# The last product of each column block in two feed-forward layers, over 128 rows of stacked weights instead of 64

## The chip, the cores and the metric

One Trainium2 chip, one core of it. The metric is the device time of one execution of the whole program in microseconds (us); lower is better. Engines are called by their short names: PE (matrix products; PEld is its loading of weights), DVE (vector), ACT (scalar), POOL (gpsimd) and SP (which issues most transfers).

## What is computed

Three layers follow one another: a linear recurrence over 768 steps for 4 batches of 8 heads, a dense feed-forward over its output, and a routed feed-forward with 8 experts.

```python
for t in range(S):                                   # 768 steps, 4 batches, 8 heads of 40
    y[:, :, t] = einsum('bhd,bhde->bhe', rt, state)
    Sa = einsum('bhde,bhe->bhd', state, at)
    state = state * wt[:, :, None, :] - einsum('bhd,bhe->bhde', Sa, bt) + einsum('bhd,bhe->bhde', vt, kt)
x = y.transpose(0, 2, 1, 3).reshape(3072, 320)
h = x @ w_in                                         # 320 -> 2048
g = where(h > 0, h, exp(min(h, 0)) - 1)
x = g @ w_out                                        # 2048 -> 320
...                                                  # gate and expert of each token
h = maximum(einsum('ecd,edf->ecf', disp, w1), 0.0)   # 8 experts, 320 -> 1024
y = einsum('ecf,efd->ecd', h, w2)                    # 1024 -> 320
out[i] = gate_w[i] * y[expert_idx[i], pos[i]]
```

## The kernel before

**Two parts of every number.** Products are made in float32r, a type of float32 width that keeps fewer digits. So that the result has float32's accuracy, an operand x is split into H (x rounded to float32r) and L (the rest), by `split`: ACT makes H, DVE makes L. A product of two split operands is wH xH + wH xL + wL xH; wL xL is left out.

**The first layer of each feed-forward.** The 320 features on the contraction side are two blocks of 128 and one of 64. For a column block of 128 hidden features the two full blocks take three products each: six. For the block of 64 the weights are stacked: `wiS` (`w1S` in the routed layer) holds wH in its rows 0 to 63 and wL in its rows 64 to 127, and x has its last 64 features twice (columns 320 to 383 repeat 256 to 319 before they are turned), so rows 64 to 127 of xH and of xL repeat rows 0 to 63. One product of `wiS` with xH over 128 rows then gives wH xH + wL xH, and one more, with xL, gives wH xL: eight products for a column block, added up in one bank of the accumulator. The dense layer's are written in `first` inside `Moe1.block` (line 581 issues them), the routed layer's in `Moe2.first` (line 901).

**Stages.** In the first 224 us or so weights are converted and the first chunks of the recurrence prepared. Then `body` goes through 12 pairs of chunks (a chunk is 32 steps of all 32 heads). In pair p it weaves together the recurrence of the two chunks (`chain`, `pre`, `inverse`: many small products in PE tiles of 32, 40, 64 or 104 rows, with DVE, ACT and POOL between them and transfers through memory) and `Moe1.block(p - 1)`, the dense layer on 256 tokens of the pair before: 16 column blocks f, each `first(f)`, then for its successors `second` with lines 595 to 597. After the last pair come its block alone, the first 256 tokens of expert 0 (`early`), and the eight experts (`expert`), each 8 column blocks of up to 448 tokens (`first`), then 3 or 4 groups of tokens (`second`, lines 907 to 909, and lines 1000 and 1001 for a group of 64), whose rows `put` scatters to the output with POOL's indirect transfers. Rows of the next expert's tokens are gathered by POOL too (line 941) and turned by PE (line 962).

**Order.** A scheduler places the instructions of every engine in a fixed order when the program is built (`ahead` lifts the recurrence over the dense layer), and each engine runs its own list in that order, waiting on semaphores of the others. So a product that could run early stands still behind one that waits.

The lines of `first` that the change touches, and those that issue the products:

```python
            for kt in range(2):
                seq += [(self.wiH[:, kt, fs], xH[:, kt]), (self.wiH[:, kt, fs], xL[:, kt]),
                        (self.wiL[:, kt, fs], xH[:, kt])]
            seq += [(self.wiS[:, fs], xH[:, 2]), (self.wiS[0:64, fs], xL[0:64, 2])]
            for i, (l, r) in enumerate(seq):
                nc.tensor.matmul(h, l, r, start=i == 0, stop=i == len(seq) - 1)
```

Of the kernel before, what the change touches and what calls it, by code (L numbers as in the profile page):

```python
# [30 lines left out]
S0 = 448  # L31
EARLY = 256
# [6 lines left out]
class Attention:  # L39
    """Chunks of 32 steps of the recurrence, all 32 heads at a time.  # L40

    In a chunk, with W the running product of w, A = W(t-1) a, Bt = b / W, Kt = k / W:
    (I + T) P = A S0' + M V with T, M the strictly lower parts of A Bt', A Kt';
    Y = W(t-1) (R S0 - low(R P') Bt + low(R V') Kt); S = (S0 - P' Bt + V' Kt) W(end).
    """

# [79 lines left out]
    def lanes(self, g, eng, eng2=None, room=None):  # L126
        """Running products and scaled operands of chunks 4g..4g+3: a lane is a chunk of a head.

        W holds 1, w, ... and then the reciprocals, running backward; room: a second such tile,
        and tiles for b and k."""  # L130
        nc = self.nc
# [22 lines left out]
        yield  # L154
        # products in 4 blocks of 8, then of the blocks
        eight = lambda t: t.rearrange("p (q r) d -> p q r d", r=8)
# [49 lines left out]
    def load_heads(self, t, src, hg, s0, n):  # L206
        """Rows of an input, n steps on partitions, the 16 heads of half hg side by side."""
        self.nc.sync.dma_start(
            t[:, :, 0:40], src[2 * hg:2 * hg + 2, :, s0:s0 + n, :].rearrange("b h s d -> s (b h) d"))

    def load_tok(self):
        """The next operand that is turned, rows of 16 heads."""
        if self.loaded == len(self.order):
            return
        kind, i = self.order[self.loaded]
        t = self.t("tok", self.loaded)
        self.loaded += 1
        for hg in range(2):
            rows = t[64 * hg:64 * hg + 64]
            if kind == "r":  # L220
                self.load_heads(rows, self.src["r"], hg, 64 * i, 64)
            elif kind == "a":
                for cc in range(2):
                    lane = (2 * (i % 2) + cc) * 32 + 16 * hg
                    self.nc.sync.dma_start(  # L225
                        rows[32 * cc:32 * cc + 32, :, 0:40],
                        self.scr_A[i // 2][lane:lane + 16].rearrange("l s d -> s l d"))
            else:
                lane = (i % 4) * 32 + 16 * hg
                self.last = self.nc.sync.dma_start(  # L230
                    rows[:, :, 0:40], self.scr_BK[i // 4][lane:lane + 16].rearrange("l x d -> x l d"))
# [28 lines left out]
    def pre(self, p):  # L260
        """Scaled operands of chunks 2p, 2p+1, features on partitions; T and M of both."""
        nc = self.nc
# [36 lines left out]
    def inverse(self, p):  # L299
        """(I + T)^-1 of chunks 2p, 2p+1, transposed: a lane for the even, one for the odd rows of each head and chunk."""  # L300
        nc = self.nc
# [7 lines left out]
        for j in range(31):  # L309
            # column j + 1, that the next step waits for, goes between the others' two operations  # L310
            n, m = j // 2 + 1, 30 - j
            if m:
                tv = self.t("ut", j)[:, 0:n * m].rearrange("p (a b) -> p a b", a=n)
                nc.vector.tensor_tensor(  # L314
                    tv, TL[:, j:j + 1, j + 2:32].to_broadcast([128, n, m]),
                    UL[:, 0:n, j:j + 1].to_broadcast([128, n, m]), ALU.mult,
                )
            col = UL[:, 0:n, j + 1]
            nc.vector.scalar_tensor_tensor(col, UL[:, 0:n, j], TL[:, j, j + 1:j + 2], col, ALU.mult, ALU.add)  # L319
            if m:  # L320
                nc.vector.tensor_tensor(UL[:, 0:n, j + 2:32], UL[:, 0:n, j + 2:32], tv, ALU.add)  # L321
            if j % 2 == 1:
                yield
# [24 lines left out]
    def bank(self, c):  # L348
        """Three banks by turns; the third has other work in the first chunks."""
        self.banks += 1  # L350
        return self.psum("r" if c >= 6 and self.banks % 3 == 0 else "c")

    def warm(self, c):
        """Products of constants, so that the tensor engine's clock stays up in the first chunks."""
        if c < 2:
# [5 lines left out]
    def chain(self, c, put):  # L361
# [12 lines left out]

        # S' and what is left of the last chunk come first
        if cc == 0:
# [91 lines left out]
def split(nc, H, L, x, low=None):  # L468
    """x = H + L: H rounded to float32r, L the rest."""
    split.last = nc.scalar.copy(H, x)  # L470
# [3 lines left out]
class Moe1:  # L474
# [9 lines left out]
    def weights(self, pool, route):  # L484
        """float64 words to float32r parts, a column block at a time; w_out w_gate beside w_out."""
        nc = self.nc
# [64 lines left out]
    def put_x(self, ident, psum):  # L551
        """x of a chunk, [tokens, features], to features on partitions, in two parts."""
        nc = self.nc
# [11 lines left out]
    def block(self, p, done):  # L565
        """Tokens of chunks 2p, 2p+1; done(c, psum) takes what comes out, [tokens, features]."""
        nc = self.nc
# [4 lines left out]
        def first(f):  # L572
# [3 lines left out]
            for kt in range(2):  # L576
                seq += [(self.wiH[:, kt, fs], xH[:, kt]), (self.wiH[:, kt, fs], xL[:, kt]),
                        (self.wiL[:, kt, fs], xH[:, kt])]
            seq += [(self.wiS[:, fs], xH[:, 2]), (self.wiS[0:64, fs], xL[0:64, 2])]
            for i, (l, r) in enumerate(seq):  # L580
# [34 lines left out]
class Router:  # L615
    """Expert and gate of each token, and each expert's list of tokens."""

# [37 lines left out]
    def settle(self):  # L655
        """From here on tokens take places from EARLY on: what is before stays as it is."""
        nc = self.nc
# [46 lines left out]
    def counts(self):  # L704
        """Places of each expert, the most of any of them."""
        nc = self.nc
# [10 lines left out]
    def overflow(self, ctx, w1, w2, out, psum):  # L717
        """Experts with more than S0 tokens: the rest of their tokens, 128 at a time."""
        nc, tc = self.nc, self.tc
# [39 lines left out]
    def drop(self, ctx, out, psum, capacity):  # L759
        """Tokens that come after their expert's capacity is filled get zeros."""  # L760
        nc, tc = self.nc, self.tc
        pool = ctx.enter_context(tc.tile_pool(name="drop", bufs=1))
        t = lambda shape, name, dt=F32: pool.tile(shape, dt, tag=name, name=name)
        # [k, m] = 1: same batch, earlier step; same batch; earlier batch
        step, same, less = t([128, 128], "step", BF16), t([128, 128], "same", BF16), t([128, 128], "less", BF16)
# [32 lines left out]
class Moe2:  # L798
# [20 lines left out]
    def weights(self, e):  # L819
        """Weights of an expert in two parts."""  # L820
        nc = self.nc
# [22 lines left out]
    def early(self, ctx, psum):  # L844
        """The first EARLY places of expert 0, in the room of expert 1's weights."""
        nc = self.nc
# [9 lines left out]
        nc.gpsimd.memset(xs, 0.0)  # L856
        # rows that are still to come
        for b in range(B):
# [34 lines left out]
    def first(self, f, h, w, xH, xL):  # L893
# [3 lines left out]
        for k in range(2):  # L897
            seq += [(w1H[:, k, fs], xH[:, k]), (w1H[:, k, fs], xL[:, k]), (w1L[:, k, fs], xH[:, k])]
        seq += [(w1S[:, fs], xH[:, 2]), (w1S[0:64, fs], xL[0:64, 2])]
        for i, (l, r) in enumerate(seq):  # L900
# [24 lines left out]
    def groups(self, e):  # L925
        """Number, first place and size of the groups of places of an expert that are still to be done."""
        return [(j, at, n) for j, (at, n) in enumerate(SLOTS) if e or at >= EARLY]

    def load(self, e):
        """Token list of an expert, and the rows of those tokens."""  # L930
        nc = self.nc
# [16 lines left out]
    def turn(self, e):  # L948
        """Rows of an expert, features on partitions, in two parts."""
        nc = self.nc  # L950
# [18 lines left out]
    def expert(self, e, turn, weights):  # L969
# [5 lines left out]
        hs = self.pool.tile([128, NF2, 2 * S0], F32R, tag="hs", name="hs", bufs=2)  # L975
        # the second part begins with the last 64 places
        hH, hL, hM = hs[:, :, 0:S0], hs[:, :, S0 + 64:2 * S0], hs[:, :, S0:S0 + 64]
# [8 lines left out]
        if turn is not None:  # L986
            drain(turn)
        # the pair that takes an addition not last of all
        for j, at, n in g if e + 1 < E else g[:1] + g[3:] + g[1:3]:
# [5 lines left out]
            else:  # L995
                # both parts of h side by side: the halves of y are added up
                w2H, w2L = w[3:5]
# [18 lines left out]
def ahead(tc, g, offset):  # L1016
    """The generator's instructions, offset places earlier for the scheduler."""
    while True:
# [8 lines left out]
def weave(*gens):  # L1027
    """Runs generators side by side, each (generator, steps[, first step]) at its own pace, all to their end."""
    state = [[g, n, at[0] if at else 0, True] for g, n, *at in gens]
# [168 lines left out]
```

## Time and profile before

| | |
|---|---|
| median of 3 runs | 1390.91 us |
| lowest and highest run | 1386.13 and 1399.85 us |
| span of the profiled execution, first to last instruction | 1384.7 us |
| median run less that span | 6.2 us |
| busy PE, PEld, DVE, ACT, POOL | 1122.0, 958.8, 780.7, 606.7, 315.7 us |
| mean granted clock of PE | 0.909 of full speed |

No separate time of the profiled execution stands beside its span; the runs' median is 6.2 us above it, and that is taken as what lies around the span. A busy share says how long an engine had something under way, not that it worked at its peak: matmuls overlap, the start of each is recorded, and its end is modelled. What a product costs in a dense stretch is therefore read from the time between the starts of neighbours (called a pitch below), and not from its duration.

### The profile page before, as it was taken

How to read it: one execution, taken by the hardware profiler on the slowest of the kernel's cores; microseconds unless marked ns; L12 is line 12 of the kernel's file. 1: busy time of each engine (PE TensorE's matmuls, PEld its weight loads, DVE VectorE, ACT ScalarE, POOL GpSimd, SP SyncE). 2: the span in 40 equal slices, each digit the busy share in tenths (PEclk: the TensorE clock that was granted, in tenths of full speed). 3: DMA queues.
4: the chain of work that ended last, by engine and by line, in shares of the span. 5: the costliest groups of instructions: out<-in, count | busy, mean ns of one | idle time of the engine just before them, and what ended most of it. 6: DMA issues, size and time to landing. Idle time of an engine off the chain costs nothing.

```text
span 1384.7 us, 35744 instructions
## 1 busy us (share of the span) xinstructions
PE 1122.0 (81%) x14568; PEld 958.8 (69%) x14568; DVE 780.7 (56%) x2632; ACT 606.7 (44%) x1498; POOL 315.7 (23%) x392
## 2 busy tenths in 40 slices
PE   0414765867679857999999999989988899999995
PEld 0313654756567756878888888878877788887884
DVE  3446674676635914785958667675444436544441
ACT  0313343445345434654656565646554325433420
POOL 4324343234123131122110110101001132223211
PEclk9999776887879978998999999999999769999998
DMA  3946765554446364345353443421020136634210
GB/s 104 202 98 134 159 131 132 133 138 96 113 107 114 94 125 100 65 96 109 60 86 73 70 83 55 76 38 41 16 85 20 30 106 168 180 113 116 73 35 18
DMA packets 316609, 131.23 MB, mean 95 GB/s; under 512 B 281468, under 2 KB 299012, under 8 KB 316436
## 3 DMA queue, kind: packets, MB, share of 16 engines
q1 hardware_dynamic: 311892, 118.73, 39.3%
q0 software_dynamic: 3584, 7.90, 2.0%
q8 instruction: 117, 1.92, 0.6%
q10 hardware_dynamic: 960, 2.23, 0.6%
q14 instruction: 56, 0.46, 0.1%
HBM read 99.13 MB, written 31.00 MB: 94 GB/s over the span
## 4 chain that ended last, share of the span: by engine, by line
PE 48%; DMA 24%; DVE 8%; SPq 8%; issue 7%; POOL 2%; ACT 2%; POOLq 0%; ACTq 0%; DVEq 0%
PE ps_h L581 11%; DMA raw<-in_moe_w_in_dram 6%; PE ps_o L595 5%; PE ps_c L373 4%; PE ps_c L901 3%; PE ps_h L901 3%; PE ps_o L596 3%; PE ps_o L597 3%; DMA out_dram<-ys,ids 3%; DMA inv<-Td 2%; PE ps_r L373 2%; DMA raw<-in_moe_w_out_dram 2%; DMA lx<-in_k_dram 2%; SPq L225 2%; SPq L138 1%
## 5 line engine op out<-in xcount | busy, mean ns | idle before, releaser
L595 PE MATMUL ps_o<-woH,gH 128*128 128x328 f32 x384 | 141.0, 369 | 1.1 <-ACT gH L470 1.1
L587 DVE SCALAR_TENSOR_TENSOR e<-e,ps_h 128x256 f32<-128x256 f32 x184 | 76.4, 417 | 114.7 <-ACT e L586 111.8
L581 PE MATMUL ps_h<-xH,wiH 128*128 128x256 f32 x368 | 115.2, 315 | 18.3 <-DVE e L587 17.7
L470 ACT CAST gH<-e 128x256 fp32r<-128x256 f32 x192 | 77.0, 405 | 110.5 <-DVE e L587 101.4
L596 PE MATMUL ps_o<-woL,gH 128*128 128x328 f32 x384 | 123.8, 324 | 0.0
L597 PE MATMUL ps_o<-woH,gL 128*128 128x328 f32 x384 | 118.0, 328 | 3.1 <-DVE gL L471 3.1
L314 DVE TENSOR_TENSOR ut<-inv 128x30 f32<-128x30 f32 (+4 forms) x360 | 100.5, 279 | 34.2 <-DMA inv<-Td 32.9
L581 PE MATMUL ps_h<-xL,wiH 128*128 128x256 f32 x368 | 110.6, 301 | 0.0
L581 PE MATMUL ps_h<-xH,wiL 128*128 128x256 f32 x368 | 109.5, 298 | 0.0
L585 ACT ACTIVATE e<-ps_h 128x256 f32<-128x256 f32 x184 | 70.4, 384 | 84.2 <-PE ps_h L581 68.8
L471 DVE TENSOR_TENSOR gL<-e,gH 128x256 fp32r<-128x256 f32 x192 | 81.9, 430 | 39.5 <-ACT gH L470 36.9
L419 POOL TENSOR_TENSOR ST<-ST,WCT 40x320 f32<-40x320 f32 x46 | 36.6, 800 | 254.2 <-DVE ST L418 88.7
L319 DVE SCALAR_TENSOR_TENSOR inv<-inv 128x1 f32<-128x1 f32 (+15 forms) x372 | 93.1, 250 | 0.5
L321 DVE TENSOR_TENSOR inv<-inv,ut 128x30 f32<-128x30 f32 (+4 forms) x360 | 91.5, 254 | 0.1
L581 PEld LDWEIGHTS ps_h<-xH,wiH 128*128 128x128 f32 x368 | 74.0, 202 | 23.4 <-DVE e L587 19.0
L595 PEld LDWEIGHTS ps_o<-woH,gH 128*128 128x128 f32 x384 | 74.8, 195 | 19.6 <-ACT gH L470 1.5
L498 DVE SCALAR_TENSOR_TENSOR x<-x,raw 128x256 f32<-128x256 f32 (+1 forms) x40 | 22.1, 552 | 114.6 <-ACT x L497 114.4
L244 PE MATMUL ps_p<-ident,tok 128*104 128x128 f32 x288 | 54.6, 319 | 38.5 <-DMA tok<-scr_A 16.0
L497 ACT ACTIVATE x<-raw 128x256 f32<-128x256 f32 (+1 forms) x40 | 18.2, 455 | 147.9 <-DMA raw<-in_moe_w_in_dram 96.3
L586 ACT ACTIVATE e<-e 128x256 f32<-128x256 f32 x192 | 79.3, 417 | 4.5
L596 PEld LDWEIGHTS ps_o<-woL,gH 128*128 128x128 f32 x384 | 75.4, 196 | 0.4
L581 PEld LDWEIGHTS ps_h<-xL,wiH 128*128 128x128 f32 x368 | 75.1, 204 | 0.8 <-issue 0.4
(302 smaller groups left out, 2993.8 us busy)
## 6 DMA issues: line engine op xcount, KB each, us to landing
r<-in_moe_w_dram SPq DMA_DIRECT2D x15, 640.0 KB
tok<-scr_BK SPq DMA_DIRECT2D x48, 160.0 KB
BKd<-scr_BK SPq DMA_DIRECT2D x48, 160.0 KB
r<-in_moe_w_dram SPq DMA_DIRECT2D x7, 1024.0 KB
W<-in_w_dram SPq DMA_DIRECT2D x10, 640.0 KB
scr_BK<-lx SPq DMA_DIRECT2D x10, 640.0 KB
inv<-Td SPq DMA_DIRECT2D x24, 256.0 KB
raw<-in_moe_w_out_dram SPq DMA_DIRECT2D x16, 320.0 KB
```

Of the source, the lines that this page charges most:

```text
L314: nc.vector.tensor_tensor(tv, TL[:, j:j + 1, j + 2:32].to_broadcast([128, n, m]), UL[:, 0:n, j:j + 1].to_broadcast([128, n, m]), ALU.mult,)
L319: nc.vector.scalar_tensor_tensor(col, UL[:, 0:n, j], TL[:, j, j + 1:j + 2], col, ALU.mult, ALU.add)
L321: nc.vector.tensor_tensor(UL[:, 0:n, j + 2:32], UL[:, 0:n, j + 2:32], tv, ALU.add)
L373: self.anchor = nc.tensor.matmul(o, l, r, start=start, stop=stop, skip_group_check=True)
L470: split.last = nc.scalar.copy(H, x)
L471: return (low or nc.vector).tensor_tensor(L, x, H.bitcast(F32), ALU.subtract)
L581: nc.tensor.matmul(h, l, r, start=i == 0, stop=i == len(seq) - 1)
L586: nc.scalar.activation(e, e, AF.Exp, scale=-1.0)
L595: nc.tensor.matmul(o, gH[:, ts], self.woH[:, f], start=f == 0, stop=False)
L596: nc.tensor.matmul(o, gH[:, ts], self.woL[:, f], start=False, stop=False)
L597: nc.tensor.matmul(o, gL[:, ts], self.woH[:, f], start=False, stop=f == NF - 1)
L901: self.nc.tensor.matmul(h, l, r, start=i == 0, stop=i == len(seq) - 1)
```

## The change

The eighth product of a column block runs over all 128 rows: `wiS` (or `w1S`) with xL, both whole. It adds wL xL for the 64 last features, which the kernel before leaves out. The diff has two such lines; everything else in it is comments and docstrings that were emptied, so that lines keep their numbers.

```diff
@@ Moe1.block, first @@
-            seq += [(self.wiS[:, fs], xH[:, 2]), (self.wiS[0:64, fs], xL[0:64, 2])]
+            seq += [(self.wiS[:, fs], xH[:, 2]), (self.wiS[:, fs], xL[:, 2])]
...
@@ Moe2.first @@
-        seq += [(w1S[:, fs], xH[:, 2]), (w1S[0:64, fs], xL[0:64, 2])]
+        seq += [(w1S[:, fs], xH[:, 2]), (w1S[:, fs], xL[:, 2])]
```

No instruction is added, removed or moved: on each of the five engines the built programs list the same instructions with the same waits in the same order. The operands were complete before: one instruction writes all 128 rows of xL, and the seventh product reads all 128 rows of the stacked weights.

## Rows read from the trace of the kernel before

**Rows 1.** Stretches: length, busy PE, PEld, DVE, ACT, POOL; clock; DMA share, GB/s.
```profile
224.00:398.00 174.00, 124.67 (x1694) 106.54 (x1695) 105.60 (x357) 68.23 (x189) 63.06 (x70) 0.76 0.50 119
398.00:548.00 150.00, 120.31 (x2002) 102.37 (x2002) 73.78 (x252) 68.17 (x176) 35.85 (x47) 0.88 0.52 110
548.00:1016.00 468.00, 451.50 (x7849) 391.90 (x7848) 321.01 (x1262) 270.66 (x697) 54.67 (x69) 0.98 0.38 71
1016.00:1081.00 65.00, 59.03 (x347) 51.85 (x348) 29.30 (x90) 34.27 (x94) 4.72 (x6) 0.89 0.09 28
1081.00:1115.00 34.00, 29.36 (x161) 25.91 (x160) 13.40 (x49) 7.94 (x23) 8.72 (x8) 0.80 0.07 17
1115.00:1356.00 241.00, 235.67 (x1174) 193.61 (x1174) 115.83 (x248) 93.92 (x165) 61.77 (x61) 0.94 0.39 113
```

**Rows 2.** Waits of PE, 548 to 1081 us: sum in us, times, longest.
```profile
PE ps_c L373 <- DVE GN L431: 5.6, 2, 4.1
...
PE ps_o L595 <- ACT gH L470: 0.8, 1, 0.8
```

**Rows 3.** Waits of PE, 1081 to 1385 us.
```profile
PE ps_p L907 <- DVE ys L994: 2.3, 1, 2.3
```

**Rows 4.** Order of time on PE, routed layer: start us, duration us, instruction.
```profile
1205.13 0.37 PE L901 MATMUL ps_h<-x2H,w1S 128*128 128x448 f32 x1
1205.43 0.46 PE L901 MATMUL ps_h<-x2L,w1S 64*128 64x448 f32 x1
1205.82 0.47 PE L901 MATMUL ps_c<-x2H,w1H 128*128 128x448 f32 x1
1206.13 0.37 PE L901 MATMUL ps_c<-x2L,w1H 128*128 128x448 f32 x1
1206.33 0.36 PE L901 MATMUL ps_c<-x2H,w1L 128*128 128x448 f32 x1
```

**Rows 5.** Order of time on PE, dense layer.
```profile
703.70 0.28 PE L581 MATMUL ps_h<-xH,wiL 128*128 128x256 f32 x1
703.82 0.28 PE L581 MATMUL ps_h<-xH,wiS 128*128 128x256 f32 x1
704.03 0.38 PE L581 MATMUL ps_h<-xL,wiS 64*128 64x256 f32 x1
704.34 0.42 PE L595 MATMUL ps_o<-woH,gH 128*128 128x328 f32 x1
704.59 0.31 PE L596 MATMUL ps_o<-woL,gH 128*128 128x328 f32 x1
704.75 0.31 PE L597 MATMUL ps_o<-woH,gL 128*128 128x328 f32 x1
```

**Rows 6.** Order of time on PE, products over 64 rows behind one another.
```profile
1124.60 0.41 PE L901 MATMUL ps_c<-x2L,w1S 64*128 64x192 f32 x1
1124.81 0.41 PE L901 MATMUL ps_h<-x2L,w1S 64*128 64x192 f32 x1
```

**Rows 7.** Order of time on PE, a column block of the early tokens.
```profile
1096.54 0.77 PE L901 MATMUL ps_c<-w2H,w1H 128*128 128x256 f32 x2
...
1098.83 0.58 PE L901 MATMUL ps_h<-w2H,w1H 128*128 128x256 f32 x1
```

**Rows 8.** Stretches, products of line 581 alone: busy us and count (x).
```profile
398.00:548.00 150.00, 39.91 (x201) 0.88 0.52 110
548.00:1016.00 468.00, 166.04 (x935) 0.98 0.38 71
1016.00:1081.00 65.00, 35.81 (x194) 0.89 0.09 28
```

**Rows 9.** Waits of DVE, 548 to 1016 us.
```profile
DVE ut L314 <- DMA inv<-Td: 18.3, 5, 6.4
```

**Rows 10.** Short stretches, columns as in rows 1.
```profile
1118.50:1145.80 27.30, 26.82 (x103) 23.73 (x103) 10.86 (x29) 9.73 (x21) 5.97 (x8) 0.50 0.47 141
...
906.90:910.30 3.40, 3.40 (x75) 2.86 (x72) 3.40 (x23) 0.88 (x3) 0.00 (x0) 0.50 0.28 51
```

## The prediction

> **What bounds the kernel now.** I read the stretches first [rows 1]. From 548 us on PE is nearly always occupied: 451.5 of 468 us up to 1016, 59.0 of 65 in the last block of the dense layer, 235.7 of 241 in the eight experts. Before that it is not: 120.3 of 150 us from 398 to 548 and 124.7 of 174 before, with DMA at half its share. A busy PE may still stand behind others, so the waits come next. From 548 to 1081 all waits of PE make 21.5 us in nine lines, the largest 5.6 us for DVE's masking of G, the smallest 0.8 [rows 2]; in the experts the largest is one wait of 2.3 us for a free output tile [rows 3]. So over about 800 us the pace is PE's own, and the question is what PE does with it. That is read from the pitch between starts.
>
> In an expert's first layer the pitch of two products of 448 columns is 0.20 us (1206.13 to 1206.33). Around the product over 64 rows it is 0.30 to it, 0.39 from it, and 0.31 after the product that follows [rows 4]. In the dense layer the pitch of 256 columns is 0.12 us and of 328 columns 0.16; around the 64 rows it is 0.21, 0.31 and 0.25 [rows 5]. Each such product makes three pitches long, not one. That it is the change of size and not the 64 rows that costs is seen where the scheduler put such products behind one another: 0.21 us from one to the next [rows 6], and this at a granted clock of 0.50, the 1.2 GHz level (the first line of [rows 10]). What happens inside PE at the change I don't need to know for the sum.
>
> **The change, part by part.** Nothing is added, removed or moved, so there is one term in several stretches: what a product over 64 rows costs more than one over 128 in its place, times their number, times the share of it that reaches the end.
>
> *Price of one.* Experts: from 1205.13 to 1206.13 are 1.00 us; three plain pitches of 0.205 are 0.615; 0.385 us more. Dense layer: from 703.82 to 704.59 are 0.77 us; plain would be 2 x 0.12 + 0.15 = 0.39; 0.38 us more. At the 1.2 GHz level a column block of the early tokens takes 2.29 us for its eight products [rows 7]; eight at twice the plain pitch of 256 columns are 8 x 0.24 = 1.92, so 0.37 more at least; twice the 0.38 would be 0.76; I take 0.5, nearer to the row. After the change the product has the form of the seventh beside it, whose pitch is known, so no unknown operation is added. The two edits (dense and routed) are alike in this.
>
> One page speaks against this. The Trainium skill, "TensorE: Matmul & The Clock Gate", section "LDWEIGHTS (loading the stationary operand)", says that a weight load over 32 rows takes as long as one over 128, and its closing table that a single product over 32 rows takes as long as one over 128. By that rule alone 64 rows cost what 128 do, the sum is nought, and the time stays at 1391; by the rows it is 0.38 us a piece. The two don't contradict where sizes don't change [rows 6], and the kernel has mostly the other case.
>
> *Recurrence and dense layer, 548 to 1016 us.* 935 products of line 581 at eight a block are 117 blocks [rows 8]: 117 x 0.38 = 44.5 us of PE's time. This is the ceiling. It isn't all paid: some of these products stand before the recurrence's own small tiles, where a change of size stays; and where PE comes sooner to an instruction that waits for DVE, ACT, POOL or a transfer, part of what is saved turns into waiting. DVE is the next engine, 321 of 468 us; at 468 - 44 = 424 it would be at 76%, so no engine's sum binds, but its order does: the inverse's first steps wait on a transfer for up to 6.4 us [rows 9], and the masking that PE waited for stands behind them. Floor: 15 us, a third, if the recurrence's own latency sets most pairs. I take three quarters, 33, because 450 of 468 us have no wait of PE now.
>
> *398 to 548 us.* 201/8 = 25 blocks, 9.5 us at most. PE idles for 30 of 150 us there, so most of it becomes a longer wait: I take 3. Before 398 us lie the other 26 of the 12 x 16 blocks; PE is idle there for 49 us and DMA at 0.50: between 0 and 5, I take 1.
>
> *1016 to 1081 us.* No recurrence is left; 194/8 = 24 blocks x 0.38 = 9. ACT (34 of 65) and DVE (29) have room. Between 5 and 9, I take 7.
>
> *1081 to 1115 us.* Eight blocks of the early tokens at 0.5 are 4, four of them in a dense run: between 2 and 5, I take 3.
>
> *The experts.* Seven experts x 8 blocks x 0.385 = 21.6; expert 0's eight stand in groups, so 1 more: 22.6. What could be late next: weights and gathered rows of the next expert, and the scattered output. PE has hardly a wait now [rows 3], DVE is at 116 and ACT at 94 of 241, POOL at 62. An expert gets shorter by 3.1 us of some 32, so I take 20, with 14 as the floor if waits like the one of 2.3 us come at every second expert.
>
> Sum: 33 + 3 + 1 + 7 + 3 + 20 = 67 us. The sum is made against the span of 1384.7, which becomes 1318; with the 6.2 us that the median lies above it the time is **1324 us**, 4.8% faster. All floors: 15 + 0 + 0 + 5 + 2 + 14 = 36, 1355 us. All ceilings: 44.5 + 9.5 + 5 + 9 + 5 + 22.6 = 96, 1295 us.
>
> **The rivals.** *The recurrence is the bound and PE only looks full.* The scheduler fills the waits of the recurrence with blocks of the dense layer; if the filling shrinks, the waits appear. For it: the waits that there are between 548 and 1016 are of this kind [rows 2, 9]. Against: they are 12 or so of 468 us. It gives the floors, 1355 us.
>
> *The clock pays too.* From 1118.5 to 1145.8 PE is busy 26.8 of 27.3 us and yet granted 0.50 [rows 10]. If denser work lets the clock rise halfway through, work of 14 us at 1.2 GHz takes 7: with the ceilings this gives 1288 us. For it: PE's products there are short and the changes of size leave holes between them. Against: nothing shows which of the two held the clock.
>
> *No change.* The rule above: rows don't matter, and the long pitches come from something that stays, the accumulator bank that changes after each column block, say. Then 1391. For it: the third long pitch lies between two full-size products. Against: seventh and eighth product write the same bank (ps_h in both rows), and the pitch between them is long already (0.30, 0.21) [rows 4, 5]. The change does what it says as far as the program goes: its eighth product has the seventh's shape.
>
> *Slower.* Faster blocks leave PE idle in the recurrence, and the clock falls. After the idle time that ends with the 4.1 us wait for DVE [rows 2], the clock was at 0.50 for 3.4 us in which PE was fully busy (the second line of [rows 10]): 1.7 us of work lost. Now this is rare, 0.98 of full clock over 468 us [rows 1]. It decides if it comes more than 67 / 1.7 = 40 times in the eleven pairs, some four times in each; at 50 times the time is 1391 - 67 + 85 = 1409 us. [...]
>
> **How the numbers follow.** The forecast 1324, between 1305 and 1340, gets 0.60; the recurrence as the bound (1340 to 1365) 0.20; the clock and the ceilings (1280 to 1305) 0.11; no change 0.05; slower 0.04. The likeliest is predicted: 1324. The range goes from 1290 (all ceilings and a little of the clock) to 1355 (all floors), which leaves out some 0.17. About 1% is what a measurement of this kernel can tell from no change; faster by over 1% (under 1377) takes the first three cases, 0.91; within 1% 0.05; slower 0.04.
>
> **What the changed profile would show.** If the price is right, no form 64*128 is left at lines 581 and 901, the eighth product's pitches are 0.12 and 0.20 us, and PE's busy time falls. If the shares are right, the stretch from the fourth pair to the last is shorter by 25 to 40 us with waits of PE up by some 10, and the experts by 17 to 22. If the recurrence is the bound, PE's waits for DVE (the masking, the states) grow to 30 us and more between 548 and 1000. If the clock pays, expert 0's stretch has less of the 0.50 level. The prediction is wrong above all if the full-size eighth product keeps a long pitch, or if saved time in the recurrence comes back as waiting by more than half.

## The result, and the profile after

The changed kernel took 1348.5 us (median of 4 runs, 1344.74 to 1354.36) against 1390.49 for the kernel before: ratio 0.9693, 95% interval 0.965 to 0.9736, so 42 us or 3.1% faster. The forecast was 1324, 24.5 us less. The time lies in the stated range of 1290 to 1355, but not in the band from 1305 to 1340 that was held likeliest (0.60): it lies in the one that was given to the recurrence as the bound (0.20). The span of the profiled execution went from 1384.7 to 1348.0 us.

The price of the eighth product came out as forecast. In the order of time on PE of the changed kernel (start, duration, instruction; first the routed layer, then the dense layer), which answers to [rows 4, 5]:

```profile
1177.91 0.37 PE L901 MATMUL ps_c<-x2H,w1S 128*128 128x448 f32 x1
1178.12 0.37 PE L901 MATMUL ps_c<-x2L,w1S 128*128 128x448 f32 x1
1178.32 0.37 PE L901 MATMUL ps_h<-x2H,w1H 128*128 128x448 f32 x1
1178.53 0.36 PE L901 MATMUL ps_h<-x2L,w1H 128*128 128x448 f32 x1
...
722.11 0.28 PE L581 MATMUL ps_h<-xH,wiS 128*128 128x256 f32 x1
722.23 0.28 PE L581 MATMUL ps_h<-xL,wiS 128*128 128x256 f32 x1
722.35 0.31 PE L595 MATMUL ps_o<-woH,gH 128*128 128x328 f32 x1
722.50 0.31 PE L596 MATMUL ps_o<-woL,gH 128*128 128x328 f32 x1
```

Seventh to eighth, to the next, and to the one after: 0.21, 0.20, 0.21 us where it was 0.30, 0.39, 0.31; in the dense layer 0.12, 0.12, 0.15 where it was 0.21, 0.31, 0.25. So 0.38 us a piece is gone in a run of full-size products.

Where the span went, in four stretches that hold the same work in both. Their bounds are starts on PE of the first eighth product of the first, the fourth and the eleventh block of the dense layer, the start of the last, and the end of the last product of the experts; all times in us:

| stretch | before | after | difference |
|---|---|---|---|
| up to the first eighth product | 229.8 | 234.4 | +4.6 |
| blocks 1 to 3 (early recurrence) | 312.0 | 315.3 | +3.3 |
| blocks 4 to 10 (recurrence and dense layer) | 460.2 | 442.1 | -18.1 |
| blocks 11 and 12, dense layer | 79.8 | 72.4 | -7.4 |
| early tokens and experts | 286.4 | 267.2 | -19.2 |
| tail after the last product | 16.6 | 16.5 | -0.1 |

The first line holds no changed instruction; other runs with unchanged work there took 230.5 to 234.7, so the 4.6 are scatter. The same stretches as busy sums, before and then after (columns as in [rows 1]):

```profile
541.80:1002.00 460.20, 445.98 (x7861) 387.58 (x7860) 317.24 (x1244) 266.96 (x691) 51.73 (x66) 0.97 0.38 68
1002.00:1081.80 79.80, 71.56 (x428) 62.25 (x427) 36.15 (x121) 41.87 (x113) 7.67 (x8) 0.91 0.19 54
1081.80:1368.10 286.30, 276.33 (x1409) 230.75 (x1408) 131.87 (x302) 101.69 (x189) 72.62 (x72) 0.92 0.34 98
```

```profile
549.80:991.80 442.00, 414.81 (x7860) 382.06 (x7860) 316.46 (x1244) 263.45 (x690) 52.32 (x66) 0.95 0.40 71
991.80:1064.30 72.50, 59.66 (x429) 58.56 (x428) 35.97 (x121) 40.91 (x112) 7.89 (x8) 0.91 0.22 59
1064.30:1331.50 267.20, 242.62 (x1410) 225.35 (x1408) 129.97 (x302) 100.68 (x189) 72.52 (x72) 0.95 0.37 105
```

In blocks 4 to 10 PE's idle time grew from 14.2 (460.20 - 445.98) to 27.2 us, in the experts from 10.0 to 24.6. The waits of PE in the changed kernel, blocks 4 to 10 and then the end (to be held against [rows 2, 3]):

```profile
PE ps_p L244 <- DMA tok<-scr_A: 7.8, 3, 3.4
PE ps_c L373 <- DVE GN L431: 5.9, 1, 5.9
PE ps_r L373 <- DVE GN L431: 2.6, 1, 2.6
PE ps_r L373 <- DMA UT<-Ud: 2.0, 1, 2.0
```

```profile
PE ps_p L907 <- DVE ys L994: 9.3, 2, 6.6
PE ps_o L962 <- DMA xs<-rows,ids: 5.0, 1, 5.0
PE ps_c L901 <- DVE hs L985: 4.4, 1, 4.4
PE ps_o L688 <- DVE hot L683: 3.7, 1, 3.7
```

The masking of G is late as before. Later than before are operands of the recurrence that are loaded back from memory (UT is new in the list, tok has 7.8 us), and in the experts the output tiles that DVE frees, 9.3 us where it was 2.3. For tok the kernel before had

```profile
PE ps_p L244 <- DMA tok<-scr_A: 1.1, 1, 1.1
```

Both scatter from run to run: the waits for output tiles are 4.5, 3.7 and 4.9 us in e2, e5 and e7 below, whose experts have the same cut, and e1, with the same blocks 4 to 10, has no wait for tok among its larger ones.

### The profile page after: what moved, and what is told of

Its sections match the earlier page's. It is cut to its first block, busy times and chain, and to the rows that moved or that the text cites. A ratio compares the mean times of both kernels' runs of the same rounds, so it can differ in the third digit from the quotient of the medians.

```text
span 1348.0 us, 35744 instructions
## 1 busy us (share of the span) xinstructions
PE 1033.6 (77%) x14568; PEld 944.8 (70%) x14568; DVE 775.6 (58%) x2632; ACT 600.8 (45%) x1498; POOL 316.7 (23%) x392
## 4 chain that ended last, share of the span: by engine, by line
DMA 35%; PE 27%; DVE 13%; SPq 10%; issue 9%; POOL 3%; ACT 3%; POOLq 0%; ACTq 0%; DVEq 0%
PE ps_h L581 7%; DMA raw<-in_moe_w_in_dram 7%; DMA out_dram<-ys,ids 6%; PE ps_c L373 3%; DMA inv<-Td 3%; DMA lx<-in_k_dram 3%; PE ps_o L595 3%; PE ps_o L596 2%; PE ps_o L597 2%; SPq L225 2%; DMA xs<-rows,ids 2%; DVE ut L314 2%; DVE inv L319 2%; DVE inv L321 2%; DMA raw<-in_moe_w_out_dram 2%
## 5 line engine op out<-in xcount | busy, mean ns | idle before, releaser
L581 PE MATMUL ps_h<-xH,wiH 128*128 128x256 f32 x368 | 115.1, 314 | 23.8 <-DVE e L587 23.2
L595 PE MATMUL ps_o<-woH,gH 128*128 128x328 f32 x384 | 130.4, 341 | 0.8 <-ACT gH L470 0.8
L314 DVE TENSOR_TENSOR ut<-inv 128x30 f32<-128x30 f32 (+4 forms) x360 | 103.3, 287 | 32.3 <-DMA inv<-Td 31.9
L581 PEld LDWEIGHTS ps_h<-xH,wiH 128*128 128x128 f32 x368 | 76.0, 207 | 26.9 <-DVE e L587 24.5
L595 PEld LDWEIGHTS ps_o<-woH,gH 128*128 128x128 f32 x384 | 77.9, 203 | 2.3 <-ACT gH L470 1.0
L596 PEld LDWEIGHTS ps_o<-woL,gH 128*128 128x128 f32 x384 | 78.1, 204 | 0.4
L597 PEld LDWEIGHTS ps_o<-woH,gL 128*128 128x128 f32 x384 | 74.2, 200 | 5.6 <-DVE gL L471 5.2
```

What stands on the lines that cost most here:

```text
L314: nc.vector.tensor_tensor(tv, TL[:, j:j + 1, j + 2:32].to_broadcast([128, n, m]), UL[:, 0:n, j:j + 1].to_broadcast([128, n, m]), ALU.mult,)
L595: nc.tensor.matmul(o, gH[:, ts], self.woH[:, f], start=f == 0, stop=False)
L596: nc.tensor.matmul(o, gH[:, ts], self.woL[:, f], start=False, stop=False)
L597: nc.tensor.matmul(o, gL[:, ts], self.woH[:, f], start=False, stop=f == NF - 1)
```

## The experiments

Ratios are to the kernel before on the same chip in the same runs; its median was 1386.76 us for e1 to e4, 1382.47 for e5 to e8, 1386.94 for e9 to e11. The theory at the outset: the price is right everywhere, and in the recurrence about half of what PE saves comes back as waiting. Rivals: the changed work itself slows the early stretch; the gains of the two layers come out of one reserve; the recurrence was the bound before already.

**e1, the dense layer alone.** The routed layer keeps its line:

```diff
-        seq += [(w1S[:, fs], xH[:, 2]), (w1S[:, fs], xL[:, 2])]
+        seq += [(w1S[:, fs], xH[:, 2]), (w1S[0:64, fs], xL[0:64, 2])]
```

> The eighth product over 128 rows in the dense layer alone; the routed layer keeps 64 rows. Theory (waits and clock): PE's saved time in the recurrence comes back by half as longer waits and as stretches at the 1.2 GHz level, the last block pays in full: 18 + 7 us less than before, about 1366; PE's idle time and its 1.2 GHz time between the fourth block's start and the recurrence's end rise by some 12 and 17 us as in the changed kernel. Rival (the change itself makes the first 550 us slower): the fourth block starts at 548 to 552 us here, and at 540 to 543 in the run with the routed layer alone.

1361.38 us, ratio 0.9794 (0.9729 to 0.986), 25 us less by the medians. Blocks 4 to 10 took 441.4, the last two 72.7 us, as in the changed kernel. The fourth block starts at 548.0 us here and at 544.7 in e2, where the rival asked for 548 to 552 and for 540 to 543: half a hit, and the first stretch alone scatters by 4 us. Its waits of PE in blocks 4 to 10:

```profile
PE ps_c L373 <- DVE GN L431: 7.0, 2, 5.3
PE ps_c L244 <- DVE ST L418: 2.8, 1, 2.8
...
PE ps_r L373 <- DMA UT<-Ud: 2.2, 1, 2.2
```

PE's idle time in these blocks rose as expected (14.2 before, 29.1 here). The part of the theory about the clock fell: stretches at the 1.2 GHz level made 22.5 us of these blocks, against 23.8 before and 40.7 in the changed kernel, and the blocks took the same time. What rose with the cut in every run was waiting.

**e2, the routed layer alone.** The other line, in the same way.

> The eighth product over 128 rows in the routed layer alone. Theory: the experts are PE's own work but for a few waits for free output tiles: 19 us less than before, about 1371, and with the dense layer alone the two add up to the whole change within 5 us. Rival (the two gains share one reserve, such as the clock): the two alone add up to more than 50 us.

1367.54 us, ratio 0.9858 (0.9795 to 0.992), 19 us less. By the medians 25 and 19 make 44, by the ratios 29 and 20 make some 48, where the whole change made 42; each is known to some 9 us. So no common reserve is needed, but the times alone don't exclude the rival's 50. The stretches speak for adding up: blocks 4 to 10 are the same in e1 as in the changed kernel, and the experts took 261.3 us against 279.8 in e1 on the same chip, 18.5 less, where the whole change made 19.2. Blocks 1 to 3 took 312.6 here as before (312.0), and 315.5 in e1: the small loss there goes with the dense layer's cut.

**e3, half of the dense blocks.**

```diff
-            seq += [(self.wiS[:, fs], xH[:, 2]), (self.wiS[:, fs], xL[:, 2])]
+            seq += [(self.wiS[:, fs], xH[:, 2]), (self.wiS[0:128 - 64 * (f % 2), fs], xL[0:128 - 64 * (f % 2), 2])]
```

> As the changed kernel, but every second column block of the dense layer keeps 64 rows; instructions and order unchanged. Theory (a reserve that is used up): the first half of the dense layer's cut pays more than the second, 1352 to 1357. Rival (a fixed part of every saved us is lost): the middle between the changed kernel and the one with the routed layer alone, 1359 to 1361.

1352.92 us, ratio 0.9735 (0.968 to 0.979). By the medians the first half pays 14.6 us and the second about 9 (the changed kernel is 0.9693 x 1386.76 = 1344 here); but the rival's middle, (0.9693 + 0.9858) / 2 = 0.9776, lies inside the interval, and in blocks 4 to 10 the profiles go the other way (458.8, 452.3, 441.4; the profiled execution of e3, 1359.79 us, was its slowest of five). It doesn't decide between a reserve that is used up and a fixed share that is lost.

**e4, two more changes of size.** In the dense layer the eighth product has 64 rows again and the third one too:

```diff
-                        (self.wiL[:, kt, fs], xH[:, kt])]
+                        (self.wiL[:, kt, fs], xH[:, kt]) if kt else (self.wiL[0:64, kt, fs], xH[0:64, kt])]
...
-            seq += [(self.wiS[:, fs], xH[:, 2]), (self.wiS[:, fs], xL[:, 2])]
+            seq += [(self.wiS[:, fs], xH[:, 2]), (self.wiS[0:64, fs], xL[0:64, 2])]
```

> Routed layer as in the changed kernel; in the dense layer the eighth product keeps 64 rows and the third one too (wL xH of the first 128 features loses the lower 64 of its features), so each block changes size twice more; instructions and order unchanged. Theory (before the change PE set the pace in the recurrence): 192 blocks get 0.38 us longer and nearly all of it counts from the fourth block on, 45 to 60 us above the run with the routed layer alone, about 1421. Rival (the recurrence's latency sets the pace there before and after): no more than the 25 us that the cut gave, about 1395.

1423.1 us, ratio 1.0252 (1.0178 to 1.0327): 56 us above e2, where taking one pair of changes a block away gave 25 or less. So before the change PE's work did set the pace in the recurrence: that PE only looked full there is out. The stretch of blocks 4 to 10, 38 us longer than in e2, has PE full:

```profile
558.70:1055.70 497.00, 488.46 (x7861) 400.67 (x7860) 320.49 (x1244) 267.16 (x691) 51.29 (x66) 0.98 0.35 63
```

Set beside e1, e2 and e3, this run shows the two sides of blocks 4 to 10. I split their time into pitches of PE over 0.35 us (a wait, nearly always: plain ones at full clock are 0.15 us and less, those at a change of size up to 0.31) and the rest:

| blocks 4 to 10, us | e4 (more) | e2 (as before) | e3 (half) | e1 (all) |
|---|---|---|---|---|
| pitches up to 0.35 us: PE's own pace | 477.9 | 437.2 | 425.0 | 403.8 |
| pitches over 0.35 us: waiting | 19.1 | 21.6 | 27.3 | 37.7 |
| together | 497.0 | 458.8 | 452.3 | 441.4 |

More work for PE is paid nearly in full, 38.2 of 40.7; less work gives 33.4 us of pace, and 16.1 come back as waiting. The same split of the kernel before and the changed one is 439.3 and 20.9 us, then 406.8 and 35.3.

**e5, 96 rows.** Both layers' eighth product over rows 0 to 95:

```diff
-            seq += [(self.wiS[:, fs], xH[:, 2]), (self.wiS[:, fs], xL[:, 2])]
+            seq += [(self.wiS[:, fs], xH[:, 2]), (self.wiS[0:96, fs], xL[0:96, 2])]
```

> As the changed kernel, but the eighth product of both layers runs over 96 rows (part of wL xL is left out; instructions and order unchanged). Theory A (PE has tiles of 32, 64 and 128 rows, and only a change of tile costs): 96 rows use the tile of 128, pitches 0.12 and 0.20 us around it, time as the changed kernel, about 1346. Theory B (any number of rows other than the neighbours' costs): pitches 0.21, 0.31, 0.25 and the time of the kernel before, about 1388.

1331.22 us, ratio 0.9681 (0.9608 to 0.9753), as the changed kernel's 0.9693. The order of time on PE, routed layer:

```profile
1150.41 0.37 PE L901 MATMUL ps_c<-x2H,w1S 128*128 128x448 f32 x1
1150.62 0.37 PE L901 MATMUL ps_c<-x2L,w1S 96*128 96x448 f32 x1
1150.82 0.31 PE L907 MATMUL ps_p<-w2H,hs 128*128 128x320 f32 x1
```

0.21 and 0.20 us: 96 rows beside 128 cost nothing. In the dense layer the two pitches are 0.12 us. So a number of rows that differs from the neighbours' isn't enough to cost anything; what fits the rows is that 64 and 128 are different kinds of tile and 96 is of the kind of 128.

**e6, 64-row products side by side.** The kernel before, odd column blocks of the routed layer in reverse order:

```diff
-        for i, (l, r) in enumerate(seq):
+        for i, (l, r) in enumerate(seq[::-1] if f % 2 else seq):
```

> The kernel before with the routed layer's odd column blocks in reverse order, so that two products over 64 rows of neighbouring blocks stand side by side; the scheduler places a few instructions anew. Theory (the change of size costs, not the 64 rows): from one 64-row product to the other 0.20 us as between full ones, long pitches only into and out of the pair, three pairs of eight blocks: some 8 us less than the kernel before. Rival (64 rows are slow in themselves): pitches of 0.3 to 0.4 inside the pair too, no gain.

One run, 1373.27 us, 9 less than the median of the kernel before on this chip, of whose seven runs two took 1371.86 and 1373.54; the experts' stretch 272.6 us, less than the 286.4 and 279.8 of runs with the routed layer unchanged. One run doesn't settle the gain. The pair, in order of time on PE:

```profile
1140.21 0.37 PE L901 MATMUL ps_h<-x2H,w1S 128*128 128x448 f32 x1
1140.51 0.47 PE L901 MATMUL ps_h<-x2L,w1S 64*128 64x448 f32 x1
1140.82 0.37 PE L901 MATMUL ps_c<-x2L,w1S 64*128 64x448 f32 x1
1141.12 0.47 PE L901 MATMUL ps_c<-x2H,w1S 128*128 128x448 f32 x1
1141.42 0.36 PE L901 MATMUL ps_c<-x2H,w1L 128*128 128x448 f32 x1
1141.62 0.37 PE L901 MATMUL ps_c<-x2L,w1H 128*128 128x448 f32 x1
```

Neither side had the pitches right: inside the pair it is 0.31, not 0.20. But from 1140.21 to 1141.42 are 1.21 us for four pitches, 0.39 over 4 x 0.205, and this for two products of 64 rows, where a single one costs 0.385. So a change of tile kind costs 0.195 us each way, paid half in the pitch of the change and half in the next; 64 rows in themselves cost nothing. What is different at a change can be seen in the order of time of PEld, in the same place:

```profile
1140.51 0.18 PEld L901 LDWEIGHTS ps_h<-x2L,w1S 64*128 64x128 f32 x1 [0.25 <-issue]
1140.62 0.19 PEld L901 LDWEIGHTS ps_c<-x2L,w1S 64*128 64x128 f32 x1
1141.11 0.19 PEld L901 LDWEIGHTS ps_c<-x2H,w1S 128*128 128x128 f32 x1 [0.31 <-issue]
1141.22 0.19 PEld L901 LDWEIGHTS ps_c<-x2H,w1L 128*128 128x128 f32 x1
```

At both changes the weights are loaded only when their product starts (1140.51, 1141.11); where the tile stays the load starts 0.20 us ahead of its product (1140.62 for 1140.82, 1141.22 for 1141.42). It is so at all 91 changes of this run at line 901: the load starts within 3 ns of its product. Such a load takes 0.18 or 0.19 us, close to the price of 0.195; that the one is the other is not shown.

**e7 and e8, the waits in the experts.** Two edits of the changed kernel:

```diff
-            ys = self.pool.tile([128, DM], F32, tag="ys", name="ys", bufs=2)[0:n]
+            ys = self.pool.tile([128, DM], F32, tag="ys", name="ys", bufs=4)[0:n]
```

> The changed kernel with four output tiles in the experts instead of two; order unchanged. Theory (the waits for DVE at the output tiles come from gathered rows that land late and hold up DVE's queue): no change, within 3 us of the changed kernel, and waits of PE for the output tiles of 5 us and more stay. Rival (two output tiles are too few, the scatter holds them): these waits go, 7 to 9 us less, about 1338.

```diff
-        ids = self.pool.tile([128, 4], I32, tag="ids2", name="ids2", bufs=3)
+        ids = self.pool.tile([128, 4], I32, tag="ids2", name="ids2", bufs=8)
```

> The changed kernel with eight tiles for the token lists instead of three, so that the list of the next expert, and the gather behind it, need not wait for an earlier expert's scatter; the scheduler then places the experts' instructions anew. Theory (late gathers are what PE waits for in the experts): the transfers of lists no longer wait for scatters, PE's waits in the experts fall from 17 us to under 8, 6 to 10 us less than the changed kernel, about 1338. Rival (the waits move elsewhere): within 3 us of it.

Four output tiles: 1333.59 us, ratio 0.9665 (0.9612 to 0.9717), which is the changed kernel's within the intervals; waits for the output tiles stay (4.9 us, longest 2.6). Eight list tiles: 1325.58 us, ratio 0.9596 (0.9538 to 0.9653), 6 and 8 us less than e5 and e7 by the medians, 12 and 10 by the ratios; the intervals still overlap, but the stretch of the experts, the only one that differs by more than some 3 us, took 250.2 us against 257.4 and 256.8. Not all of these 7 us are waiting: PE's idle time in the stretch was 12.9 us against 15.5 in both, and the time at the 1.2 GHz level 13.7 us against 20.5. What held the output tiles is seen in DVE's order of time in the changed kernel:

```profile
1234.52 0.69 DVE L835 TENSOR_TENSOR w1S<-r,w1T 64x512 fp32r<-64x512 f32 x1
1244.84 0.17 DVE L957 COPY gate<-xs 128x4 f32<-128x4 f32 x1 [9.63 <-DMA xs<-rows,ids]
1244.95 0.55 DVE L994 TENSOR_SCALAR ys<-ps_p,gate 128x320 f32<-128x320 f32 x1
```

DVE stood for 9.63 us at the copy of the next expert's gates, for rows that the gather hadn't brought, and the product's tile waited behind it. The gather needs its token list, and that transfer waited for the scatter of an earlier expert, since three list tiles go round. In all DVE waited 37.5 us for gathered rows in the stretch, six times; in e8 14.2, three times. SP's waits, changed kernel and then e8:

```profile
SPq L938 <- DMA out_dram<-ys,ids: 34.3, 8, 7.2
...
SPq L938 <- DMA list<-ids,idx: 10.8, 1, 10.8
```

```profile
SPq L816 <- DVE w2L L471: 15.2, 6, 3.1
SPq L938 <- DMA list<-ids,idx: 10.7, 1, 10.7
```

The eight waits for the scatter are gone, and with them PE's waits for output tiles; its waits in the stretch are

```profile
PE ps_o L962 <- DMA xs<-rows,ids: 5.2, 1, 5.2
PE ps_o L688 <- DVE hot L683: 3.7, 1, 3.7
PE ps_c L901 <- ACT x2H L470: 3.0, 1, 3.0
```

With a wait of 0.9 us for the routing they make 12.8 us, and 8.2 without the routing's two (L688), where under 8 were expected. The scheduler placed the experts' instructions anew in e8, which may have a part in it.

**e9 to e11, DVE relieved.** Every second rest gL of the dense layer on POOL:

```diff
-            split(nc, gH, gL, e)
+            split(nc, gH, gL, e, nc.gpsimd if f % 2 else None)
```

> The changed kernel with the rest gL of every second column block of the dense layer made by POOL instead of DVE (96 of 192 subtractions of 0.43 us; the scheduler places instructions anew). Theory (what PE waits for in the recurrence now is DVE's queue): DVE's sum there falls by some 25 us of 319, PE's waits there shrink by a third or more, 5 to 12 us less than the changed kernel. Rival (the latency of transfers and of round trips between engines is the wait, DVE's queue is not): within 4 us of it, or slower, since a subtraction on POOL takes longer.

e10 is e8 with four output tiles and the gates copied by POOL:

```diff
-        nc.vector.tensor_copy(gate[:, js], xs[:, js, DM])
+        (nc.gpsimd if e else nc.vector).tensor_copy(gate[:, js], xs[:, js, DM])
```

> The eight list tiles, with four output tiles and with POOL instead of DVE copying the gates of the gathered rows. Theory (late gathers were the wait, and earlier lists have cured it): within 4 us of the run with eight list tiles alone (0.960 of the kernel before). Rival (DVE's queue still stands behind the gathered rows): 4 to 8 us less, 0.954.

e11 has the edits of e8 and e9:

> Eight list tiles and every second gL on POOL together. If both relieve different stretches, their gains add: the experts' 10 to 13 us of the list tiles and whatever the run with gL on POOL alone shows, 0.952 to 0.960 of the kernel before. If gL on POOL gives nothing: 0.960.

e9: 1369.26 us, ratio 0.9882 (0.9842 to 0.9923), slower than the changed kernel by 26 us on the ratio; e11: 1354.52, 0.9796 (0.9748 to 0.9843), slower than e8 by as much. e10: 1337.92, 0.9658 (0.9617 to 0.9698), 8 or 9 us slower than e8 on the ratio, where the theory asked for 4 at most and the rival for a gain: both missed. Its experts took 256.2 us, as in e7, though it has the list tiles of e8; e11, which has them too, took 250.1. So what the list tiles are worth isn't settled. e11 missed both of its expectations too. In e9 blocks 4 to 10 took 463.1 us; DVE's waits from 549 to 1005 us:

```profile
DVE e L587 <- ACT e L586: 64.2, 45, 6.9
DVE ut L314 <- DMA inv<-Td: 32.8, 7, 13.2
```

In the changed kernel these two are 49.8 and 14.8 us. So taking 24 us of subtractions from DVE made nothing earlier: DVE stood longer for ACT and for the inverse's transfer. This speaks against DVE's sum as what PE waits for, but doesn't show it: the scheduler placed much anew in e9, and a subtraction took 0.74 us on POOL where it took 0.43 on DVE. The loss itself isn't explained.

## Why the prediction was right, and where it was off

**The price was right.** 0.38 us a product in both layers, and the change of tile as its cause: pitches of the changed kernel, e5 and e6. The Trainium skill, "TensorEngine Tiling (Array Packing)", section "Key Properties", says that a switch of the tiling mode drains PE; its section "Available Configurations" has modes of 32, 64 and 128 rows and none of 96. The runs fit both: 0.195 us for each switch, with the weights loaded late (e6), and nothing for 96 rows (e5). The rule that rows don't matter holds inside one mode [rows 6], and the rival "no change" that was made of it is out. For the early tokens at the 1.2 GHz level 0.5 us was taken against twice the plain pitch at full clock; the plain pitch in the same place is 0.21 us (1097.12 to 1097.33), which gives 2.29 - 8 x 0.21 = 0.6, under 1 us more over eight blocks.

**Last blocks and experts: near, the experts in part by luck.** The 7 were forecast for the last 24 column blocks; these took 58.9 and then 53.1 us, 5.8 less (the 7.4 of the table hold 8 more blocks). For the experts with the early tokens 23 were forecast; it was 19.2 in the profiles, 18.5 between e1 and e2, 19 in the runs of e2. But the 19.2 are a net: PE's busy time fell by 33.7 us (276.3 to 242.6). Of that some 8.5 are the clock's, an estimate from 17.1 us less at the 1.2 GHz level at half speed; that leaves 25 for the cut. PE's waiting grew by 14.6. The clock's gain and the waiting, neither in the sum, partly cancelled. What was named as late next did come: one wait of 2.3 us became 9.3, behind a late gather (e8; less in other runs).

**The recurrence: the term that was mis-sized.** The prediction paid 33 of a ceiling of 44.5 us in blocks 4 to 10, because PE had hardly any wait there. Measured were 18.1. These blocks are 112 of the 117, with 42.6 at most; counted up to the last 24, 120 blocks, it was 19.7. Two steps of it were off. The ceiling: where the recurrence's small tiles come next, a switch stays, which the text said but left out of its 44.5. By the order on PE that is so for 11 of the 112, some 4 us; but PE's own pace fell by only 33.4 us (e2 against e1), and the rest of that gap is open. And the share: three quarters were taken, one half came, as 16.1 us returned as waiting, in pieces of a few us at DVE's masking, at states that DVE adds up (e1), at operands from memory. By the prediction's own signs the stretch should have been 25 to 40 us shorter, which it wasn't, and more than half of the saved time coming back would have made it wrong above all: 16.1 of 33.4 is just under half. A PE that is full says that more work costs all of it (e4); it doesn't say that less work gives it back, since waits that are just covered don't show. The rival "the recurrence is the bound" named these waits, and its 15 us for this stretch were nearer than the 33 taken; but that PE only looked full, its premise, is refuted (e4). That the time fell into its band is no proof of it.

**Before 548 us: the sign was off.** 3 + 1 us of gain were taken; blocks 1 to 3 took 3.3 us more. The stretch lasted 313.1 to 317.2 us in eight profiles with the dense layer cut (310.7 in e9, whose order differs) and 311.5 to 312.6 in the three without; in e4, with more work, it took 325.4. PE idles there anyway, 78.8 us before and 90.7 after, for DVE, ACT, POOL and transfers, and the time at the 1.2 GHz level went from 110.6 to 131.0 us: the rival "slower" in a small way. Why the cut makes the stretch longer isn't shown; that more work does so too says that PE's work isn't without weight there. Over the profiles a longer stretch goes with more time at that level (310.7 us with 113.8, 317.2 with 132.9), but which of the two makes the other isn't shown.

**The clock rival.** It came in part. Expert 0's stretch at the 1.2 GHz level was 27.3 us in the kernel before and in e1, and 10.2 in the changed kernel; between the last block of the dense layer and the end of the experts 44.4 us became 27.3. It is part of the 19.2; a gain beyond the ceilings did not come, since waits took it. In e2 to e5, e7 and e8, with the experts cut, the sum was 13.7 to 27.3 us; in e6, uncut, 23.9, so it scatters.

In the sum: 33 + 3 + 1 + 7 + 3 + 20 = 67 us was forecast; the profiles give 18.1 - 3.3 + 7.4 + 19.2 + 0.1 = 41.5 from the first changed product on, and the runs 42. The 6.2 us that were added for what lies around the span were mostly scatter too: in every run with both numbers the time is 1.7 to 2.0 us above the span.

What stays open: which of the recurrence's waits stands behind the others. A third tile for the operands that are loaded back would have tried the waits for tok; it wasn't tried.

## What to carry to other kernels

A product over few rows among products over many is dear by its neighbours, not by itself: look at the pitches of the one before and the two behind it, and fill the rows (with a harmless term; here 96 of 128 did as well as 128) or put such products side by side, which here halved the price a product (the gain in time isn't settled, e6). When a full engine gets less to do, don't count on all of it: here it was about half where PE's work is woven into a chain of other engines, and some three quarters in the experts, where it nearly runs alone. Adding work and taking it away are two different measurements. And after a gain look at what waits newly: here it was the token lists, with a gain of half to one per cent in e8 that e10 didn't repeat.

## What was not expected of the hardware

A change of tile kind costs in two pitches, 0.09 us in that of the change and 0.105 in the one behind, so that a pair of 64-row products shows 0.30, 0.31, 0.30, 0.30 (e6). At the 1.2 GHz level PE stayed for 27.3 us although it was busy for 26.8 of them [rows 10]; products of 192 columns followed one another there at 0.21 us [rows 6], no faster than those of 256 columns at that level (1097.12 to 1097.33).
